# Loading the second batch's values in three pieces with tiny transfers between them

## The chip, the cores and the metric

The kernel runs on one core of a Trainium2 chip. The metric is the device time of one execution in microseconds; lower is better. Five engines work side by side: PE (TensorE, matmul), DVE (VectorE), ACT (ScalarE), POOL (GpSimd) and SP (SyncE). Sixteen DMA engines move data between HBM and the on-chip memory of 128 partitions. In this kernel POOL issues nearly all transfers, in the order of the program.

## The reference, cut to what matters

```python
# q, k, v: [8, 8, 576, 64] f32, 8 batches, 8 heads
scores = q @ k.T / 8
mask   = rel in [0, 32)                        # heads 0..3
         rel in [0, 128) and rel % 4 == 0      # heads 4..7
attn   = softmax(where(mask, scores, -1e9)) @ v
x      = attn as [4608, 512]                   # batch and position by head and dimension
logits = x @ phi                               # 32 slots: 8 experts by 4
slot_input = softmax(logits over rows).T @ x   # [32, 512]
for e in 8 experts:
    slot_out[e] = relu(slot_input[e] @ w1[e]) @ w2[e]     # 512 -> 1024 -> 512
out    = softmax(logits over slots) @ slot_out            # [4608, 512] f32
```

The values `v` of batch 1 are what the change loads in another way. `phi` is a small table of 512 by 32.

## The kernel before, in words

Everything is held in f16 on the chip; q, k, v and the weights lie in HBM as f32 and are converted on their way in, by the transfer itself. Such transfers are issued from POOL.

Attention goes batch by batch. `load_raw` (line 197) fetches Q, K or V of one batch into a tile of 128 partitions by 2304 elements: 64 rows of (head, 16 position blocks), each with two groups (the plain heads and the dilated heads), so that partition 2r + g holds row r of group g. One partition is 9216 contiguous bytes in HBM. Each of Q, K and V has two buffers. DVE transposes a raw tile in two halves (`turn`, line 223) into `qT`, `kT` or `vT`; PE makes the scores (line 273), ACT the exponentials (line 282), DVE multiplies the masks in (line 293), PE multiplies with the values (line 316), and DVE and ACT normalise (lines 328, 337, 341). A written-out list, `ORDER` (line 48), fixes the order of these steps over the batches, a few stages deep; nothing is moved by a scheduler. `logits` and the slot sums are gathered as each batch is done.

The order of the loads is fixed as well. Lines 460 to 476 issue Q and K of batch 0, V of batch 0, Q and K of batch 1, `phi_raw` and V of batch 1. From then on `loads` (line 527) issues a batch's Q, K or V two batches ahead, as soon as DVE has turned the tile whose buffer it takes; after V of batches 3 to 7 it adds one transfer of `w1` each, and after the last one all of the weights that fit: `w1` of experts 5 to 7 and `w2` of experts 0 to 2, 3 MB each as it lies on the chip. When the raw tiles are done with, `w2` of experts 3 to 5 follows (line 555), and experts 6 and 7 by halves of the columns (`load_half`, line 216).

The experts come after the last batch: PE makes the hidden layer (line 608) and `slot_out` (`emit_so`, line 635). The first halves of the columns are finished first, `so_part` is copied out of PSUM (line 652), spread and copied (line 658), and then the outputs are made: PE (line 664), ACT or DVE (lines 673, 677), and a transfer to HBM (line 686), batch by batch for the first half of the columns, then for the second, then whole rows for batches 6 and 7 and for the last 64 positions of all batches (line 713).

A transfer reports its end on one of eight completion counters, which are taken in turn. In the built program an issue on POOL waits until the transfer that used the same counter before it has landed.

Of the kernel before, what the change touches and what calls it, by code (L numbers as in the profile page):

```python
# [10 lines left out]
FP16 = mybir.dt.float16  # L11
# [16 lines left out]
N_SLOTS = 32  # L28
# [3 lines left out]
PJ = S // PB  # L32
# [12 lines left out]
    (("P", 3), ("P", 4), ("L", 0), ("L", 1), ("D", 0)),  # L45
    (("D", 1), ("D", 2), ("D", 3)),
)
ORDER = """
MD0.2 MK2.2 AP4.2 ET.3 VBc.1 S1.1 MK0.1 RP4.2 ED.3 E1.1 AD1.2 EP.3 VC.1 RD1.2 MP4.2
VCc.1 ER.3 MD1.2 AD3.2 VA.1 QT0.0 AP3.2 RD3.2 VAc.1 QT1.0 RP3.2 MD3.2 S2.1 KT1.0  # L50
# [3 lines left out]
"""  # L54
STEPS = [(w.split(".")[0], int(w.split(".")[1])) for w in ORDER.split()]
ON_ACT = ('D3', 'P0', 'P1', 'P3')
# [40 lines left out]
def kernel(  # L97
# [10 lines left out]
    nc = tc.nc  # L108
# [5 lines left out]
    consts = ctx.enter_context(tc.tile_pool(name="consts", bufs=1))  # L114
# [3 lines left out]
    ident = cst[:, o : o + 128]  # L118
    spread = cst[:, o + 128 : o + 256]
    quad = cst[:, o + 256 : o + 260]  # L120
    masks = consts.tile([128, NMASK], FP16, name="masks")
    phi_raw = consts.tile([128, 4, N_SLOTS], FP16, name="phi_raw")
    phi4 = consts.tile([128, 4, 4, N_SLOTS], FP16, name="phi4")
# [59 lines left out]
    def build_masks():  # L183
# [8 lines left out]
        for kind, i in GROUPS[1]:  # L192
            w = piece_w(kind, i)
            copies(o, lmask[i] if kind == "L" else band, w, 1)
            o += w

    def load_raw(which, b):
        t = raw_pool.tile([128, PJ * D], FP16, name=f"raw{which}_{b}", tag=f"raw{which}")
        raw[(which, b)] = t
        src = {"Q": q, "K": k, "V": v}[which][b]  # L200
        nc.gpsimd.dma_start(  # L201
            out=t, in_=src.rearrange("(g h) (p j) d -> (h p) g (j d)", g=2, j=PJ)
        )

    def load_full(t, which, e0, e1):
        if which == 1:
# [253 lines left out]
    for which in "QK":  # L460
        load_raw(which, 0)
# [3 lines left out]
    for i in range(2):  # L465
        nc.vector.memset(vX[i][:, :, :, D : D + 1], 1.0)
        for x in (xp_t[i], xd_t[i]):
            nc.vector.memset(x[:, :, 4 * D : 4 * D + 1], 1.0)
    load_raw("V", 0)
    for which in "QK":  # L470
        load_raw(which, 1)
    nc.gpsimd.dma_start(
        out=phi_raw.rearrange("p (u c) s -> p u (c s)", u=2),
        in_=moe_phi.rearrange("(u p c) s -> p u (c s)", u=2, c=2),
# [65 lines left out]
    for it in range(B + max(s for _, s in STEPS)):  # L540
        for op, stage in STEPS:
            b = it - stage
# [16 lines left out]
        if it == 0:  # L559
            nc.vector.tensor_copy(  # L560
                out=phi4, in_=phi_raw[:, :, None, :].broadcast_to([128, 4, 4, N_SLOTS])
# [55 lines left out]
    for c in range(8):  # L617
# [3 lines left out]
        out=hTm[:, 0].rearrange("p c (j s) -> p c j s", j=4)[:, :, :, 0:16], in_=hT4[:, :, :, 0:16]  # L621
    )
    nc.scalar.copy(
        out=hTm[:, 1].rearrange("p c (j s) -> p c j s", j=4)[:, :, :, 16:32], in_=hT4[:, :, :, 16:32]
# [87 lines left out]
    for e in range(2):  # L712
        nc.gpsimd.dma_start(
            out=rest[:, e, 512:576, :].rearrange("n i d -> i n d"), in_=om_l[64 * e : 64 * e + 64]
# [37 lines left out]
```

## Time and profile before

| | |
|---|---|
| runs | 178.04, 178.28, 178.61 us; median 178.28 |
| the profiled execution | 178.29 us; span 176.5 us |
| PE busy | 123.5 us (70%), 2004 matmuls |
| DVE busy | 126.0 us (71%) |
| ACT busy | 123.5 us (70%) |
| POOL busy | 38.4 us (22%) |
| DMA | 40.83 MB in 18981 packets; 62.07 MB read from HBM, 9.44 MB written |
| chain that ended last | ACT 38%, DMA 27%, DVE 14%, PE 10% |

The span is the time from the first to the last instruction in the profile; 1.8 us lie around it. The page cuts the span into 40 slices and gives, for each, the busy share of the engines in tenths and the mean busy share of the sixteen DMA engines. The chain of waits is followed back from the last instruction: at each step to what released it. The trace also keeps the times at which each transfer's sixteen shares were reported done, one by each DMA engine, and the start and length of every DMA packet, both without the engine's number. Queue q0 holds the transfers of POOL, q1 that of SP; q8 and q14 hold instructions that the engines' sequencers fetch.

### The profile page before, as it was taken

The numbers are of one execution on the slowest core, as the hardware profiler recorded it, in microseconds if no ns is written. First come the engines' busy times: TensorE is split into PE (matmuls) and PEld (weight loads), VectorE is DVE, ScalarE is ACT, GpSimd is POOL, SyncE is SP. The second block draws the span as 40 slices with busy tenths as digits, with TensorE's granted clock in tenths as the row PEclk, the third lists the DMA queues.
The fourth block names the chain that finished last, engine by engine and source line by source line (L and its number), as shares of the span: only waits on it lengthen the run. The fifth ranks groups of instructions, "written<-read, shape, count | busy, mean of one in ns | idle before, by whom it ended". The sixth has DMA issues, their size and how long they took to land.

```text
span 176.5 us, 4724 instructions
## 1 busy us (share of the span) xinstructions
PE 123.5 (70%) x2004; PEld 80.9 (46%) x2004; DVE 126.0 (71%) x275; ACT 123.5 (70%) x266; POOL 38.4 (22%) x60
## 2 busy tenths in 40 slices
PE   0026928998888888988989888978677295778300
PEld 0015616676566566656766557656332142221000
DVE  6473899999999999999999998465130104878500
ACT  6007758999999999999999999995501104888300
POOL 7321022112112112116000002710000001856600
PEclk9999999969999999999789999996858969655555
DMA  5999999999999999999999999999999999999997
GB/s 83 215 214 210 214 212 215 215 213 214 216 212 217 211 218 215 208 215 220 213 211 217 213 218 216 222 210 225 213 213 221 192 198 175 340 398 397 401 415 209
DMA packets 18981, 40.83 MB, mean 231 GB/s; under 512 B 1169, under 2 KB 11537, under 8 KB 18193
## 3 DMA queue, kind: packets, MB, share of 16 engines
q0 software_dynamic: 18816, 40.41, 113.8%
q8 instruction: 15, 0.25, 0.5%
q1 hardware_dynamic: 144, 0.14, 0.3%
q14 instruction: 6, 0.04, 0.1%
HBM read 62.07 MB, written 9.44 MB: 405 GB/s over the span
## 4 chain that ended last, share of the span: by engine, by line
ACT 38%; DMA 27%; DVE 14%; PE 10%; issue 2%; POOL 2%; POOLq 0%; ACTq 0%
DMA w<-in_moe_w_dram 19%; ACT p L282 10%; DMA phi_raw<-in_moe_phi_dram 8%; ACT vX L253 7%; ACT xp L337 7%; DVE qk L231 5%; PE f L664 5%; ACT om L673 3%; ACT xT L376 3%; ACT xT L378 3%; DVE p L293 3%; DVE vT L231 3%; ACT xd L337 2%; PE s L273 2%; PE rp L357 2%
## 5 line engine op out<-in xcount | busy, mean ns | idle before, releaser
L282 ACT ACTIVATE p<-s 128x1920 f16<-128x1920 f32 (+1 forms) x24 | 44.6, 1857 | 10.2 <-PE s L273 10.1
L273 PE MATMUL s<-qk 32*128 32x128 f16 (+2 forms) x704 | 26.7, 295 | 18.4 <-DVE qk L231 12.0
L253 ACT COPY vX<-rv 128x768 f16<-128x768 f16 (+1 forms) x32 | 27.8, 943 | 1.8 <-PE rv L247 1.8
L316 PEld LDWEIGHTS <-p 128*128 128x128 f16 (+1 forms) x480 | 22.4, 103 | 13.3 <-DVE xp L341 4.0
L337 ACT ACTIVATE xp<-o_P,rc_P 128x64 f16<-128x64 f32 x96 | 26.5, 497 | 2.2 <-DVE rc_P L328 2.2
L273 PEld LDWEIGHTS <-qk 32*128 32x128 f16 x704 | 17.3, 117 | 21.6 <-DVE qk L231 12.0
L293 DVE TENSOR_TENSOR p<-p,masks 128x1920 f16<-128x1920 f16 (+1 forms) x24 | 25.7, 1084 | 0.2
L231 DVE STREAM_TRANSPOSE qk<-rawQ 128x576 uint32<-128x576 uint32 x16 | 18.8, 1243 | 2.7 <-DMA rawQ<-in_q_dram 2.7
L316 PE MATMUL o_P<-vX,p 128*128 128x65 f16 (+1 forms) x288 | 20.0, 205 | 0.8 <-ACT xp L337 0.2
L231 DVE STREAM_TRANSPOSE qk<-rawK 128x576 uint32<-128x576 uint32 x16 | 19.5, 1231 | 0.4 <-DMA rawK<-in_k_dram 0.4
L247 PE MATMUL rv<-cst,vT 128*128 128x128 f16 x176 | 17.5, 242 | 3.2 <-DVE vT L231 1.8
L231 DVE STREAM_TRANSPOSE vT<-rawV 128x576 uint32<-128x576 uint32 x16 | 19.4, 1223 | 0.5 <-DMA rawV<-in_v_dram 0.5
L686 POOL DMA_DIRECT2D out_dram<-om x15 | 11.1, 744 | 39.2 <-DVE om L677 34.8
L247 PEld LDWEIGHTS <-vT 128*128 128x128 f16 x176 | 13.2, 124 | 7.5 <-issue 3.7
L677 DVE TENSOR_SCALAR om<-f,rrow 128x256 f16<-128x256 f32 (+1 forms) x28 | 13.5, 519 | 3.5 <-PE f L664 2.9
L664 PE MATMUL f<-so_sb,ET 32*128 32x256 f16 (+1 forms) x60 | 12.5, 392 | 3.9 <-ACT om L673 2.7
L673 ACT ACTIVATE om<-f,rrow 128x256 f16<-128x256 f32 (+1 forms) x28 | 12.8, 503 | 2.6 <-PE f L664 2.0
L376 ACT COPY xT<-rp 128x576 f16<-128x576 f16 x16 | 11.5, 909 | 1.3 <-PE rp L357 1.3
L316 PE MATMUL o_D<-vX,p 128*128 128x65 f16 x128 | 9.9, 202 | 2.5 <-DVE xp L341 2.0
L201 POOL DMA_DIRECT2D rawQ<-in_q_dram x8 | 5.1, 633 | 29.4 <-DVE rc_P L328 18.4
L378 ACT COPY xT<-rd 128x576 f16<-128x576 f16 x16 | 10.6, 795 | 0.0
L341 DVE TENSOR_TENSOR xd<-o_D,rc_D 128x256 f16<-128x256 f32 x24 | 9.9, 412 | 0.2
(81 smaller groups left out, 176.7 us busy)
## 6 DMA issues: line engine op xcount, KB each, us to landing
w<-in_moe_w_dram POOLq DMA_DIRECT2D x3, 3072.0 KB, 35.5
out_dram<-om POOLq DMA_DIRECT2D x11, 512.0 KB, 4.6
w<-in_moe_w_dram POOLq DMA_DIRECT2D x5, 1024.0 KB, 15.9
rawQ<-in_q_dram POOLq DMA_DIRECT2D x8, 576.0 KB, 12.7
rawK<-in_k_dram POOLq DMA_DIRECT2D x8, 576.0 KB, 11.4
rawV<-in_v_dram POOLq DMA_DIRECT2D x8, 576.0 KB, 11.6
out_dram<-om POOLq DMA_DIRECT2D x2, 1024.0 KB, 7.3
w<-in_moe_w_dram POOLq DMA_DIRECT2D x2, 512.0 KB, 36.7
```

The costliest lines, as they stand in the source:

```text
L231: nc.vector.transpose(out=out_, in_=in_)
L247: nc.tensor.transpose(rg[:, n_t, :, c, :], rows, ident)
L253: copy(out=vX[b % 2][:, t0 : t0 + n, :, 0:D], in_=rg.rearrange("p n h c d -> p n h (c d)"))
L273: nc.tensor.matmul(sps[:, h, c0 : c0 + w], kk, qq, start=(tt == 0), stop=(tt == 1))
L282: return nc.scalar.activation(out=pt, in_=sps[:, :, 0:n], func=AF.Exp, scale=SCALE)
L293: return nc.vector.tensor_tensor(out=pt, in0=pt, in1=m, op=ALU.mult)
L316: nc.tensor.matmul(o[rows, h, :], lhs, rhs, start=(n == 0), stop=(n == len(jobs) - 1), skip_group_check=True,)
L337: nc.scalar.activation(out=dst[:, h], in_=src[:, h], func=AF.Copy, scale=rc[:, h : h + 1])
L376: copy(out=xT_t[b][:, c, :], in_=rg[:, 0:S])
L378: copy(out=xT_t[b][:, 2 + c, :].rearrange("p (i r) -> p i r", r=DIL), in_=rg[:, :, 0:SUB].rearrange("p r i -> p i r"),)
L664: nc.tensor.matmul(fp[:, 0 : c1 - c0], ET[32 * j : 32 * j + 32, m : m + 128], so_sb[32 * j : 32 * j + 32, c0:c1], start=True, stop=True,)
L673: nc.scalar.activation(out=dst, in_=fp[:, 0 : c1 - c0], func=AF.Copy, scale=rrow[:, blk : blk + 1])
```

## The change

One load is written otherwise, that of V of batch 1. Its 128 partitions come as one transfer of 96 partitions (source rows 0 to 47 of 64, two groups each) and two transfers of 16 partitions (rows 48 to 55 and 56 to 63). After each of the three stands a tiny transfer that copies rows of `phi` into a new tile, `aside`, which nothing reads: 3, 8 and 5 rows by two pieces of 32 elements. The last count is worked out from the first, (-3 - 24) mod 16 = 5. All six are issued from POOL, where one was issued before; DVE's first transpose of this tile waits for all three pieces. What is computed stays the same.

```diff
+CURSOR = 3
...
+    aside = consts.tile([16, 3, 2, N_SLOTS + 16], FP16, name="aside")
...
+    def step_cursor(i, n):
+        nc.gpsimd.dma_start(
+            out=aside[0:n, i, :, 0:N_SLOTS],
+            in_=moe_phi[0 : 5 * n].rearrange("(p u) s -> p u s", u=5)[:, 0:4:2, :],
+        )
+
     def load_raw(which, b):
         t = raw_pool.tile([128, PJ * D], FP16, name=f"raw{which}_{b}", tag=f"raw{which}")
         raw[(which, b)] = t
         src = {"Q": q, "K": k, "V": v}[which][b]
-        nc.gpsimd.dma_start(
-            out=t, in_=src.rearrange("(g h) (p j) d -> (h p) g (j d)", g=2, j=PJ)
-        )
+        src = src.rearrange("(g h) (p j) d -> (h p) g (j d)", g=2, j=PJ)
+        if (which, b) != ("V", 1):
+            nc.gpsimd.dma_start(out=t, in_=src)
+            return
+        nc.gpsimd.dma_start(out=t[0:96], in_=src[0:48])
+        step_cursor(0, CURSOR)
+        nc.gpsimd.dma_start(out=t[96:112], in_=src[48:56])
+        step_cursor(1, 8)
+        nc.gpsimd.dma_start(out=t[112:128], in_=src[56:64])
+        step_cursor(2, (-CURSOR - 24) % 16)
```

## The prediction

> **What bounds the kernel now.** I read the page's slices first, then its queues, then the chain of waits.
>
> ```profile
> DMA  5999999999999999999999999999999999999997
> GB/s 83 215 214 210 214 212 215 215 213 214 216 212 217 211 218 215 208 215 220 213 211 217 213 218 216 222 210 225 213 213 221 192 198 175 340 398 397 401 415 209
> DMA packets 18981, 40.83 MB, mean 231 GB/s; under 512 B 1169, under 2 KB 11537, under 8 KB 18193
> ## 3 DMA queue, kind: packets, MB, share of 16 engines
> q0 software_dynamic: 18816, 40.41, 113.8%
> q8 instruction: 15, 0.25, 0.5%
> ```
>
> After its first slice the row of DMA shares is full: the sixteen DMA engines have work from 4 us to the end. 212 to 220 GB/s while f32 is read and f16 written, about 400 in the last slices, where f32 is written. Compute comes second: the chain of waits ends in one long DMA piece.
>
> ```profile
> 109.68 1.62 PE s L273 x24
> 111.30 0.28 issue
> 111.58 0.74 POOL w L220
> 112.33 34.05 DMA w<-in_moe_w_dram
> 146.41 0.32 PE so L641 x4
> 146.76 0.43 DVE so_part L652
> ```
>
> Attention's last scores are done at 111.3; then everything stands for 34 us until the second weight matrix is in. Its transfers were issued by 115 and only wait for their turn in the queue. So the time is the sum of what the **latest** DMA engine has to move, plus the tail. The tail goes with it:
>
> ```profile
> 149.40 3.03 POOL L686 DMA_DIRECT2D out_dram<-om  x4 [33.97 <-DVE om L677]
> ...
> 152.63 0.74 POOL L686 DMA_DIRECT2D out_dram<-om  x1 [0.19 <-issue]
> ```
>
> The first output is issued at 149.40, while the last weights land at 151.70 (landing times here and below are from the trace's update records). From there on half-MB outputs land every 1.31 us (153.14, 154.44, 155.79, ... 166.35), up to 175.23. The late engines go from weights to outputs without a gap, so a late engine's delay reaches the end in full.
>
> **The engines are not equally late.** For each transfer the trace records sixteen completion updates, one an engine (without the engine's number). How far the first is ahead of the last:
>
> ```
> transfer          last update   spread
> rawK, batch 1          17.89      0.41
> rawV, batch 1          20.93      0.45
> rawQ, batch 2          24.50      1.26
> rawV, batch 5          64.89      1.53
> w1 of experts 5..7    111.91      2.65
> last half of w2       151.70      2.65
> ```
>
> The first step falls on the first q8 packet, 16 KB of instructions that starts at 22.27 and takes 0.94 us: it holds up one engine. Following the packets' start times as sixteen chains, I find the first fourteen q8 packets on eight chains in a fixed turn, so six were hit twice by 129; the fifteenth (144.76) makes it seven. At 151.70 seven engines are within 0.43 us of the last (0, 0.20, 0.27, 0.28, 0.32, 0.41, 0.43), the other nine at least 1.48 before it. Those **seven late engines** set the time.
>
> **The change, part by part.** *Fewer engines for two pieces.* The 96-partition piece has 48 source rows of two groups, six partitions an engine, as before. The pieces of 16 partitions have 8 rows by 2 groups, and no transfer of before has fewer than 16 outer rows, so the trace doesn't show how such a one is spread. Bounds: over all sixteen (one partition each, nothing shifts), or over eight (two partitions each). I take eight, by the nearest rows: every transfer here with 64 or 128 outer rows gave each engine whole outer rows, and eight outer rows fill eight engines. Then, if each such transfer takes up where the one before ended, 3 + 8 + 8 + 8 + 5 = 32 brings the turn round: the first piece goes to engines 3 to 10, eight tiny rows to 11 to 15 and 0 to 2, the second piece again to 3 to 10, and the last five tiny rows to 11 to 15. Engines 3 to 10 carry two partitions more of V than before (the other eight two fewer).
> The Trainium skill ("DMA: Bandwidth & Descriptors", section on why a DMA increments its semaphore by 16) says so: the largest count up to 16 that divides the slowest dimension of both sides, and from GpSimd that many consecutive engines from a turning cursor; no row here shows it. By the same section some copies from GpSimd go to sixteen engines all the same; by that the shift would be nil, which is a rival below.
>
> *Price of the shift.* Batches 0 and 1 land at 6.84, 9.61, 12.43, 15.17, 17.89: 11.05 / 4 = 2.76 us for 8 partitions an engine, 0.345 each. Two of them: 0.69 us, plus on eight engines and minus on eight.
>
> *Price of five more transfers.* Each posts a completion on every engine: the 4-byte packets of q0 take 22 ns, so 5 x 0.022 = 0.11 us on all (from nothing, if they hide, up to 5 x 0.26 = 1.3, if each cost as much as phi_raw did from K's landing, 17.89 to 18.15; that one had 16 row pieces an engine as well, so I stay with 0.11). The tiny rows: 0.26 / 16 = 0.016 each, at most four on an engine of the second eight, 0.06.
> Sum: engines 3 to 10 get 0.69 + 0.11 = **+0.80**, the others -0.69 + 0.17 = **-0.52**.
>
> *V of batch 1 lands later.* 20.93 becomes about 21.7. It is first wanted here:
>
> ```profile
> 24.95 1.22 DVE L231 STREAM_TRANSPOSE vT<-rawV 128x576 uint32<-128x576 uint32 x1
> ```
>
> That is 3.2 us of cover left; for every later Q, K and V the cover is 6 us or more (Q of batch 2 lands at 24.50 and is turned at 31.10). With that cover gone, a late transpose would cost up to 0.8.
>
> *POOL and the eight counters.* Each transfer takes the next of eight completion counters, and in the built program an issue waits until the transfer eight before it has landed. With five more in line, Q of batch 2 no longer goes at 9.51 but waits for K of batch 1:
>
> ```profile
> 4.76 1.04 POOL L201 DMA_DIRECT2D rawV<-in_v_dram  x1
> 9.51 0.59 POOL L201 DMA_DIRECT2D rawQ<-in_q_dram  x1 [3.71 <-DVE qk L231]
> 12.27 0.59 POOL L201 DMA_DIRECT2D rawK<-in_k_dram  x1 [2.17 <-DVE qk L231]
> 15.09 0.59 POOL L201 DMA_DIRECT2D rawV<-in_v_dram  x1 [2.23 <-DVE vT L231]
> 22.08 0.59 POOL L201 DMA_DIRECT2D rawQ<-in_q_dram  x1 [6.40 <-DVE qk L231]
> ```
>
> So Q goes at 17.9, K behind it at 18.5, V at 20.3, when the 96-partition piece has landed; Q of batch 3 keeps its 22.1. The first transfer had packets moving at 2.68 after its issue at 1.28, 1.4 us. Q's rows are thus ready at 19.3. The relieved engines run out of V at 20.48 - 0.52, about 19.9, the others at 21.2. Margin 0.6 us: cost nothing, with up to 0.6 or so on the relieved engines if it fails.
>
> **Which engines are the late ones?** This decides the sign. If the latest engine is among 3 to 10, the end moves by +0.80. If it is not but one of the other six is, by 0.80 less 0.20 to 0.43, so +0.37 to +0.60. Only if all seven are among the relieved eight, it moves by -0.52 (the next group, 1.48 earlier, then stands at -0.68, behind). The trace gives no numbers. The eight chains are hit in an order that fits eight engines in a row; of sixteen places where such a row could start, one puts all seven into the relieved eight. Weak evidence besides: packets of equal start stand in the record in an order that never contradicts itself between two chains, and in it three chains that are never hit stand ahead of most of the eight. If that order is the engines' numbers, the row starts at 3 or above and does not wrap, and overlaps 3 to 10.
>
> **Rivals.**
> Forecast: at least one late engine is loaded, +0.37 to +0.80. I take +0.66: 178.29 + 0.66 = **178.95**. Chance 0.58.
> Other side, *the relieved eight are the late ones*: 178.29 - 0.52 = 177.77. For it: eight are hit and eight are relieved, so an exact match is possible; against it: one place in sixteen and the record's order. It decides as soon as all seven are outside 3 to 10. Chance 0.22, more than a sixteenth, since the numbering is unknown to me.
> *The change doesn't do what it says*: pieces go over sixteen engines, only five completions and the tiny rows are added, +0.11 to +0.17: 178.43. Chance 0.15.
> *The queue runs dry at Q of batch 2*, because the counters hold it to 17.9 and packets need longer than 2 us from there: all engines lose 0.5 to 1.0 at about 20 us, 179.0 to 179.3, whatever the sets. Against it: 1.4 us at the start. Chance 0.05.
>
> **Numbers.** The sum is made against the profiled execution, 178.29 (span 176.5 and 1.8 around it), next to the median of 178.28. A measurement of this kernel tells about 0.3% (0.53 us) from no change. Of the forecast's 0.58, about 0.10 lies below 178.82 and counts as same, 0.48 is slower; of the 0.22, 0.14 is counted faster and 0.08 same; the third is same; the fourth mostly slower. Faster 0.14, same 0.33, slower 0.53. The range must reach to the gain, as without it 0.22 is left out: 177.7 to 179.2. The forecast's own: 178.6 to 179.1.
>
> **What would show it.** Landing of V of batch 1: spread of about 1.8 (0.45 + 2 x 0.69) instead of 0.45 if eight engines are used; 0.45 if sixteen. POOL's issue of Q of batch 2 at 17.9 with a wait on DMA. No gap in the DMA row near 20 us. The last w2 half: first and last update; at 152.2 to 152.5 in the forecast, 151.2 in the gain. The chain's w piece longer or shorter by the same, the tail unchanged. I am wrong if these landings move and the end doesn't, or if compute waits on V of batch 1.

## The result, and the profile after

The changed kernel takes 178.97 us (median of 13 runs, 178.71 to 179.85) against 178.26 (13 runs, 177.95 to 178.71): ratio 1.0042, 95% interval 1.0026 to 1.0058. It is slower by about 0.7 us, as forecast (178.95). Its profiled execution took 179.09 us (span 177.3), the one before 178.29 (span 176.5). Six of its thirteen runs lie at 178.71 to 178.80, so what is read below from one execution at 179.09 need not hold in full for all of them. In twice_same, a run below, two of six executions were slow, near 182.5 us, and its ratio is made of the other four.

The page of the changed kernel, the rows that answer to those of before:

```profile
DMA  5999999999999999999999999999999999999997
GB/s 89 211 214 209 193 214 212 214 213 216 216 212 217 212 214 215 214 214 213 215 211 219 212 218 216 225 213 213 224 213 211 199 198 171 318 399 395 402 412 218
DMA packets 19188, 40.84 MB, mean 230 GB/s; under 512 B 1376, under 2 KB 11744, under 8 KB 18400
## 3 DMA queue, kind: packets, MB, share of 16 engines
q0 software_dynamic: 19024, 40.41, 113.5%
q8 instruction: 15, 0.25, 0.5%
```

Between its first and last slice the row of DMA shares still shows nothing but nines, but the row below it shows a change: the fifth slice (17.7 to 22.2 us) moved 193 GB/s, 214 before. The bytes are the same to 0.01 MB; 207 small packets have come in.

The end of the chain of waits of the changed kernel (start, us, what):

```profile
138.87 2.68 issue
141.55 6.13 PE so L656 x60
147.70 0.43 DVE so_part L667
148.18 0.28 PE rep L672
148.48 0.38 ACT so_sb L673
```

`so_part` is copied at 147.70, 146.76 before. In this execution PE is itself busy up to there: it ran the stretch 141 to 147 us at half the clock (granted 0.50, 0.73 before). Is PE then the cause? A run below, with the same landings, has PE free for 0.97 us ahead of them and gains nothing by it.

Landings are from the trace's update records, last update and spread of the sixteen, in us:

```
transfer                              before          after
V of batch 1, 96 partitions                           20.21  0.50
  rows 48 to 55                                       20.74  0.66
  rows 56 to 63 (before: the whole)   20.93  0.45     21.80  1.36
Q of batch 2                          24.50  1.26     25.17  1.79
w2, last of the first halves          146.37 2.66     147.29 3.25
w2, last of the second halves         151.70 2.65     152.11 2.73
last output                           175.23          176.01
```

The last output is 0.78 later, the last weights only 0.41. The first halves of the columns, for which `so_part` waits, are 0.92 later: so the loss has two parts, and the second (some 0.37 us) goes back to a landing just before 147.3. POOL's first issues of outputs in the changed kernel:

```profile
150.35 2.19 POOL L701 DMA_DIRECT2D out_dram<-om  x3 [34.00 <-DVE om L692]
152.74 0.75 POOL L701 DMA_DIRECT2D out_dram<-om  x1 [0.20 <-ACT om L688]
```

They begin 0.95 later than before (149.40). The first output packets start at 151.63, 0.48 us before the last weights are in; before it was 150.68, 1.02 ahead. Around 153.1 the DMA engines then run dry for a moment: from 152.5 to 153.5 their packets leave 0.12 us an engine unused (before 0.00), and the third output lands 1.44 us after the second (1.30 before). So a part of the second loss is seen in the packets; the rest builds up over the later outputs.

POOL's issues at the start of the changed kernel, from its timeline (in brackets the idle time ahead and what ended it):

```profile
4.80 0.96 POOL L213 DMA_DIRECT2D rawV<-in_v_dram  x1
5.33 1.01 POOL L200 DMA_DIRECT2D aside<-in_moe_phi_dram  x1
7.15 0.57 POOL L215 DMA_DIRECT2D rawV<-in_v_dram  x1 [0.81 <-DMA rawQ<-in_q_dram]
9.91 0.56 POOL L200 DMA_DIRECT2D aside<-in_moe_phi_dram  x1 [2.19 <-DMA rawK<-in_k_dram]
12.73 0.55 POOL L217 DMA_DIRECT2D rawV<-in_v_dram  x1 [2.26 <-DMA rawV<-in_v_dram]
15.48 0.58 POOL L200 DMA_DIRECT2D aside<-in_moe_phi_dram  x1 [2.21 <-DMA rawQ<-in_q_dram]
18.46 0.59 POOL L211 DMA_DIRECT2D rawQ<-in_q_dram  x1 [2.40 <-DMA phi_raw<-in_moe_phi_dram]
19.02 0.66 POOL L211 DMA_DIRECT2D rawK<-in_k_dram  x1
20.74 0.58 POOL L211 DMA_DIRECT2D rawV<-in_v_dram  x1 [1.06 <-DMA aside<-in_moe_phi_dram]
22.09 0.58 POOL L211 DMA_DIRECT2D rawQ<-in_q_dram  x1 [0.77 <-DVE qk L246]
```

By the eight counters, Q of batch 2 waits for K of batch 1 (landed at 17.90), and goes at 18.46 (9.51 before), 0.56 us later. The bracket names `phi_raw` (18.15), the landing that came last, but in no_middle, a run below, the same issue waits for Q of batch 1 (15.00) and goes at 15.55, with no other landing near. The pieces and tiny transfers follow their landings by 0.28 us (6.87 and 7.15, 15.20 and 15.48). From 22.09 on the times are those of before. The packet records show what this did: per 0.342 us, 16 rows of 9 KB should start, one an engine. From 19.37 on it is 9, 14, 10, 13, 12, 14, 15 and then 16 again (before: 16 with single 15s). 25 rows are missing, 25 x 0.345 / 16 = 0.54 us an engine on average, less what the tiny rows and the added completions took. The relieved engines' last rows of V start by 19.26 and take 0.36 us; the first rows of Q, from 19.80, take up to 1.1 us. The engines that still had pieces of V did not stop.

DVE's first transpose of this tile did not move; from its timeline:

```profile
24.96 1.22 DVE L246 STREAM_TRANSPOSE vT<-rawV 128x576 uint32<-128x576 uint32 x1
```

### The profile page after: what moved, and what is told of

Read it like the earlier page. It is cut to its first block, busy times and chain, and to the rows that moved or that the text cites. A ratio compares the mean times of both kernels' runs of the same rounds, so it can differ in the third digit from the quotient of the medians.

```text
span 177.3 us, 4730 instructions
## 1 busy us (share of the span) xinstructions
PE 124.3 (70%) x2004; PEld 80.8 (46%) x2004; DVE 125.9 (71%) x275; ACT 123.6 (70%) x266; POOL 41.3 (23%) x65
## 4 chain that ended last, share of the span: by engine, by line
ACT 43%; PE 21%; DVE 16%; DMA 8%; issue 4%; POOL 2%; POOLq 0%; ACTq 0%; DVEq 0%
ACT p L297 10%; ACT xp L352 9%; DMA phi_raw<-in_moe_phi_dram 8%; ACT vX L268 8%; DVE qk L246 5%; ACT xT L391 5%; PE f L679 5%; ACT xT L393 4%; PE so L656 4%; ACT om L688 3%; PE hps L623 3%; ACT xd L352 3%; DVE vT L246 3%; PE rv L262 2%; DVE p L308 2%
## 5 line engine op out<-in xcount | busy, mean ns | idle before, releaser
L262 PE MATMUL rv<-cst,vT 128*128 128x128 f16 x176 | 18.2, 250 | 3.1 <-DVE vT L246 1.8
L246 DVE STREAM_TRANSPOSE qk<-rawK 128x576 uint32<-128x576 uint32 x16 | 19.6, 1235 | 0.4 <-DMA rawK<-in_k_dram 0.4
L262 PEld LDWEIGHTS <-vT 128*128 128x128 f16 x176 | 13.8, 126 | 7.2 <-issue 3.8
L352 ACT ACTIVATE xd<-o_D,rc_D 128x64 f16<-128x64 f32 x32 | 9.2, 536 | 1.3 <-DVE rc_D L343 1.3
```

What stands on the lines that cost most here:

```text
L246: nc.vector.transpose(out=out_, in_=in_)
L262: nc.tensor.transpose(rg[:, n_t, :, c, :], rows, ident)
L352: nc.scalar.activation(out=dst[:, h], in_=src[:, h], func=AF.Copy, scale=rc[:, h : h + 1])
```

## The experiments

The theory behind the forecast: the latest DMA engines set the end, and some of them are among engines 3 to 10, which carry two partitions more. Its rivals: the transfers themselves cost the time, or the hold-up of Q of batch 2. Ratios are against the kernel before on the same chip, with the 95% interval.

### Without the shift: the middle tiny transfer left out, and pieces over sixteen engines

Run no_middle: the second piece begins where the first one ended.

```diff
-        step_cursor(1, 8)
...
-        step_cursor(2, (-CURSOR - 24) % 16)
+        step_cursor(2, (-CURSOR - 16) % 16)
```

> The three pieces of V and two of the three tiny transfers stay; the middle one is gone and the last has 13 rows, so the two pieces of 16 partitions go to engines 3 to 10 and then 11 to 2, two partitions to every engine. Theory (the loss is the uneven load): four more transfers than before, 4 x 0.022 = 0.09 us on every engine, so about +0.1 us against the kernel before, V of batch 1 lands with a spread near 0.5 us. Rival (the loss is the price of many transfers and of the held-up issue of Q of batch 2): +0.5 to +0.7 us, like the changed kernel.

Measured: 178.47 against 178.29, ratio 1.0016 (1.0007 to 1.0025). The second piece lands with a spread of 0.25 us, the first one in two groups of eight with 0.47: the two pieces fill up all sixteen engines. The last weights land at 151.68. Four more transfers, without the shift, leave the late landings where they were; the medians are 0.18 apart.

Run sixteen: three pieces and three tiny transfers, all of 16 or more rows.

```diff
+        nc.gpsimd.dma_start(out=t[0:64], in_=src[0:32])
+        step_cursor(0, 16)
+        nc.gpsimd.dma_start(out=t[64:96], in_=src[32:48])
+        step_cursor(1, 16)
+        nc.gpsimd.dma_start(out=t[96:128], in_=src[48:64])
+        step_cursor(2, 16)
```

> Six transfers as in the change, but each has 16, 32 or more outer rows: V as 64, 32 and 32 partitions, the tiny ones with 16 rows. Theory (uneven load): every engine keeps its 8 partitions, five more completions cost 0.11 us, so +0.1 to +0.2 us. Rival (the number of transfers and the eight counters, which hold Q of batch 2 back to 18 us, cost the time): +0.5 to +0.8 us, and the DMA engines stand idle near 20 us.

Measured: median 178.55, ratio 1.0029 (1.0009 to 1.0049; two of twelve runs lie above 179.7). Q of batch 2 is issued at 18.25 here as well, but no engine had run out of V; last weights 151.68. The hold-up by itself, with all engines equally loaded, moves no landing of the last weights (the median is 0.26 over that of before). The first halves, though, land 0.39 late (146.76); more of that below.

### Other engines loaded: counts 11 and 15

```diff
-CURSOR = 3
+CURSOR = 11
```

> The mirror image: engines 11 to 15 and 0 to 2 carry two partitions more, 3 to 10 two fewer. In the changed kernel's landings the first, sixth, seventh and eighth of the eight engines hit by code fetches were loaded and the second to fifth relieved. Theory (four of the late engines stand on either side): the latest engine is now among the loaded, +0.8 us at the last weights, and the time 0.6 to 0.9 us over the kernel before. Rival (the change only picked the wrong side): -0.5 us.

> Engines 15 and 0 to 6 carry two partitions more, 7 to 14 two fewer. Theory A (the engines hit by code fetches are a row of eight, and 3 to 10 overlapped its first four, so it is 7 to 14): all late engines are relieved, the last weights land 0.5 us earlier than before and the time is 0.3 to 0.5 us under the kernel before, less what the relieved engines lose standing idle near 20 us. Theory B (they are every second engine): four of them are loaded again, +0.5 us. Theory C (the row is 15 to 6): all are loaded, +0.8 us.

Measured: 11 gives 179.21, ratio 1.0066 (1.0040 to 1.0092), last weights 152.38 (+0.68, for 0.8 expected). 15 gives 178.73, ratio 1.0030 (1.0018 to 1.0042), last weights 152.22. So loading the other eight engines is slower too, and so is a set between them: the theory that the eight chains with the instruction fetches are eight engines in a row, which count 15 would relieve, falls. The last landings fit every second engine instead, visited in a turn: any eight in a row then hold four of them. In before the late engines end about 0.43, 0.28, 0, 0.29, 0.27 and 0.39 us ahead of the last, in the order of their first fetch (the seventh 0.4 after its second, the eighth 1.53). With 3 the groups of landings put the first, sixth, seventh and eighth among the loaded: -0.39 + 0.80 = +0.41. With 11 it is the second to fifth: 0 + 0.80; with 15 the fourth to seventh: -0.27 + 0.80 = +0.53. Measured: +0.41, +0.68, +0.52. The spread bears this out for two of the counts: with 3, three engines end within 0.01 us of each other and the next 0.50 ahead; with 11, four end within 0.13 and the next 0.77 ahead. With 15 there are no such groups (six engines within 0.18), so there the fit rests on the last update alone. The engines' numbers themselves are not in the trace.

### The dose: the shift twice, and opposed

V of batch 4 is loaded in the same way, with the count c = 3 (twice_same) or c = 11 (twice_opposed).

```diff
-        if (which, b) != ("V", 1):
+        if (which, b) not in (("V", 1), ("V", 4)):
...
+        c, i = (3, 0) if b == 1 else (11, 3)
```

> The change made twice, in V of batch 1 and in V of batch 4, with the same counts 3, 8, 5: engines 3 to 10 carry four partitions more. Theory (late engines that carry more set the end, and half of those that fetch are among them): two shares of 0.80 on a late engine that was 0.39 ahead of the last: last weights at 151.70 - 0.39 + 1.60 = 152.9, with a spread of over 4 us, and the time 179.5 to 180.0 (178.3 + 1.2, and up to 0.5 more by the fetch). Rival (what costs is the hold-up of Q of batch 2 by the completion counters at 18 to 21 us, which batch 4 does not have): the second time adds no more than its five transfers, 179.0 to 179.2.

> The same ten transfers more as in the run with the change made twice, but with the counts 11, 8, 13 in V of batch 4, so that engines 11 to 2 carry the two partitions more there: over both, every engine carries what it carried before. Theory of the late engines: only the transfers remain, 2 x 0.11 to 2 x 0.17 us: 178.5 to 178.65 (up to 178.9 if the fetch comes in between), the spread of the last weights back to 2.6. Rival (the hold-up at 18 to 21 us costs): 179.0 to 179.3, since V of batch 1 is as in the changed kernel.

Measured: twice_same has ratio 1.0073 (1.0057 to 1.0089), 179.60 in the profiled execution, last weights at 152.94 (152.9 expected) with a spread of 3.98. The dose is as the theory has it, and the rival (only transfers added) falls. Its chain shows the weights longer by that much:

```profile
112.29 30.00 DMA w<-in_moe_w_dram
142.31 5.69 PE so L657 x59
```

The piece of DMA ends at 142.29, when w2 of experts 3 to 5 is in; 141.10 before.

twice_opposed missed the theory's figure: ratio 1.0054 (1.0039 to 1.0069), median 179.28, last weights 152.88. The opposed shift did not cancel. Either the second set was not the complement of the first, or the relief of the first had been lost. The landings speak for the second. At Q of batch 2 the engines of after without a fetch stand in two groups: seven around 24.12 and eight around 23.5, where before all stood around 23.45. The loaded ones are thus +0.67, in place of +0.80, and the relieved ones +0.05, in place of -0.52.

### The same away from the hold-up

late_opposed makes the two opposed shifts in V of batches 4 and 5, batch4_only the single shift in batch 4.

```diff
-        if (which, b) != ("V", 1):
+        if (which, b) not in (("V", 4), ("V", 5)):
```

> The pieces and tiny transfers in V of batches 4 and 5 in place of batch 1, counts 3, 8, 5 and then 11, 8, 13: engines 3 to 10 carry two partitions more by the one and two fewer by the other. Theory H: in the run with batches 1 and 4 the opposed shift did not cancel, because in batch 1 the eight relieved engines stood idle from 19.5 to 21.5 us until Q of batch 2 was issued, so that their relief was lost (+0.07 in place of -0.52 at 25 us) and only the load of the others remained. Here the queue is full, so the two shifts cancel and only ten transfers remain, 2 x 0.11 to 2 x 0.17 us: last weights at 151.9 to 152.05 with a spread of 2.5 to 2.8, 178.5 to 178.65 us (up to 0.3 more if the 15th fetch falls into the first half's last weights). Rival G (the second set of engines is not the complement of the first: the turn does not stand at 0 at batch 4): last weights over 152.4 and 179.1 to 179.5, as in that run.

> The change's six transfers with 3, 8, 5 in V of batch 4 in place of batch 1, so no queue runs dry. Theory (late engines 0.39 behind the last are loaded): last weights at 151.70 - 0.39 + 0.80 = 152.1, 178.7 to 179.0, and the late engines among the relieved keep their relief: they end 0.9 to 1.2 ahead of the last (0.6 in the changed kernel). Rival (the hold-up of Q of batch 2 is what costs): 178.35 to 178.45, only the transfers being left.

Measured: late_opposed has its last weights at 151.92 with a spread of 2.61, as theory H said; the rival G needed over 152.4. So the sets are complements, and ten transfers cost 0.22, 0.022 each. The profiled execution took 178.58, as expected, but the median is 178.76, above it: the eight runs lie in two groups, 178.50 to 178.58 and 178.94 to 179.08, ratio 1.0028 (1.0016 to 1.0040).

batch4_only: 178.80, ratio 1.0035 (1.0023 to 1.0047), last weights 152.22 (+0.52; 0.41 was expected). Without any hold-up the shift costs the same, so the rival (178.35 to 178.45) falls. Behind three engines within 0.24 of the last, the next end 0.85 ahead of it (0.9 to 1.2 expected for the relieved ones, 0.50 in the changed kernel), which fits engines that kept their relief. The medians say less than the landings: ten balanced transfers (178.76) cost about as much as five with the shift (178.80). That the shift is what costs rests on the traced executions. Its chain of waits:

```profile
113.02 33.91 DMA w<-in_moe_w_dram
146.93 0.04 issue
146.97 0.32 PE so L656 x4
```

The first halves land at 146.93, 0.56 later than before, and the last output at 175.74, 0.51 later: here all three move by one amount, as the forecast had it. In the changed kernel they do not.

### The second part: PE's 15th instruction fetch

In the changed kernel this fetch (145.19) comes while its engine still has rows of the last of the first halves to move; the engine's share lands 1.5 us later than by its place among the others, 0.49 us after all of them. One transfer later it is delayed by 1.0 only. To shift the fetch, 32 PE instructions were added (after_code, before_code) or left out (after_less, before_less, whose hidden layer lacks a quarter of its rows) in a stretch where PE waits for weights anyway.

```diff
-    for c in range(8):
+    for c in 3 * list(range(8)):
         nc.tensor.transpose(hT[:, c, :], h_sb.rearrange("p (q l) -> p l q", l=8)[:, c, :], ident)
```

> The changed kernel, with the eight PE transposes of the hidden layer (hT, at about 138 us) done three times over: 32 PE instructions more, in a stretch in which PE waits for weights, so that PE's 15th instruction fetch (16 KB on q8, at 145.19 us) is asked for one to two microseconds earlier in the weights. Theory T: of the +0.92 us by which the last weights of the first half of the columns are later (147.29 for 146.37), 0.49 are not the shift of partitions but that fetch, which reaches its DMA engine while the engine still has a piece of this transfer to do; the end follows this landing. Then without the coincidence it lands at 146.8 to 146.9, the last weights stay at 152.1, and the time is 0.3 to 0.5 below the changed kernel's: 178.5 to 178.7, against 178.3 before. Rival R: the place of the fetch is of no account and the tail follows the last weights (152.11) or the compute: 178.9 to 179.0.

> The kernel before with the same 32 PE instructions more. In it the 15th fetch reaches its engine when that engine is through with the first half's last weights (it is 1.5 us ahead), so both theories expect no change: 178.2 to 178.4, the last weights of the first half at 146.4 and the last of all at 151.7. It tells what the added instructions cost by themselves.

Measured: before_code 179.19, ratio 1.0048 (1.0034 to 1.0062); after_code 180.19, ratio 1.0126 (1.0087 to 1.0165). Both expectations missed, for a reason that I had not thought of. The page of before_code:

```profile
GB/s 89 208 216 209 215 216 212 215 215 212 214 215 217 211 213 218 214 212 216 215 213 214 216 214 226 217 211 218 222 209 216 194 197 167 386 398 392 405 414 139
...
q8 instruction: 16, 0.26, 0.5%
```

There are 16 fetches, and the last one comes at 161.25, among the outputs. The last weights are not late (151.46), fifteen engines report the last output from 174.48 to 174.97 (before: from 174.64 on), and the sixteenth 0.97 us after them, at 175.94: a spread of 1.46 in place of 0.59. The kernel is slower by that. It is the plainest proof in this study that the latest engine sets the end: 1.07 us of one engine, where none has slack, cost 0.8. For the question asked the pair is of no use: in after_code the 15th fetch came at 145.04, hardly earlier, and the first halves at 147.10.

```diff
-            for dc in range(4):
+            for dc in range(3):
```

> The changed kernel with 32 PE instructions fewer: the hidden layer is summed over three quarters of its 512 rows (the last quarter's 16 matmuls and 16 weight loads are left out), at about 131 to 136 us, where PE is ahead of the weights. PE's 15th instruction fetch then comes later in the weights than at 145.19 us, and no 16th comes (the run with 32 more got one at 162 us, on an engine without slack, and lost 0.8 us by it). Theory T: the fetch reaches its engine when that is through with the last weights of the first half; these land at 146.8 (147.29 with the fetch in between, 146.37 before), and the time is 178.5 to 178.75. Rival R (the place of the fetch is of no account): 178.9 to 179.0.

> The kernel before with the same 32 PE instructions left out (hidden layer over three quarters of its rows). Both theories: 178.2 to 178.4, first half at 146.4, last weights at 151.7; it tells what leaving them out does by itself.

Measured: before_less 178.21, ratio 0.9998 (0.9989 to 1.0007). after_less 178.81, ratio 1.0035 (1.0023 to 1.0047); the fetch came at 145.18, not later, and the first halves at 147.28. So neither pair moved the fetch in the changed kernel by more than 0.15 us, and theory T was not put to the test that I meant. after_less does settle PE's share; from its timeline:

```profile
141.55 4.80 PE L656 MATMUL so<-w,hTm 128*32 128x512 f16 x57 [2.69 <-issue]
147.32 0.29 PE L656 MATMUL so<-w,hTm 128*32 128x256 f16 x4 [0.97 <-DMA w<-in_moe_w_dram]
```

PE stood idle for 0.97 us and then waited for the landing all the same, at a ratio within the interval of the changed kernel's (1.0042). The landing is the bound there, not PE.

What remains is a comparison over the profiled executions, without the two that had a sixteenth fetch. The fetch shows as a spread that is larger in the last of the first halves than in the transfer ahead of it:

```
                spread ahead, of it   last weights   last output   difference
after           2.72  3.25            152.11         176.01        23.90
sixteen         2.49  2.92            151.68         175.45        23.77
cursor11        3.07  3.64            152.38         176.30        23.92
after_less      2.54  3.07            152.08         175.93        23.85
before          2.65  2.66            151.70         175.23        23.53
no_middle       2.59  2.56            151.68         175.15        23.47
cursor15        2.56  2.62            152.22         175.71        23.49
twice_same      3.98  4.01            152.94         176.47        23.53
twice_opposed   3.52  3.56            152.88         176.43        23.55
late_opposed    2.61  2.64            151.92         175.46        23.54
batch4_only     3.14  3.18            152.22         175.74        23.52
before_less     2.47  2.49            151.52         175.10        23.58
```

In the four with the larger spread the end comes 23.77 to 23.92 after the last weights, in the eight others 23.47 to 23.58, whatever else was changed. So some 0.3 to 0.4 us of the loss go with that coincidence. That it is the cause is shown by no run that makes or takes it away alone; that stays open. The two groups of late_opposed, 0.5 us apart, would fit it, but only one execution was traced.

## Why the prediction was right, point by point

**The latest DMA engine sets the end.** Held: a double dose gave +1.24 on the last weights (+1.21 by the sum), and one fetch among the outputs 0.8 us at the end.

**Eight engines for a piece of 8 rows by 2.** Held. The pieces land in two groups of eight (0.66, then 1.36 of spread; 1.8 was forecast), and without the middle transfer they balance to 0.25. The Trainium skill ("DMA: Bandwidth & Descriptors", "Why a DMA increments its semaphore by 16 and not by 1") states both the eight engines and the turning start, and these landings agree with it. Its exception, sixteen engines for some copies, did not come up.

**Two partitions, 0.69 us, and five transfers, 0.11.** Held in the main: together +0.67 on the loaded engines at Q of batch 2, for 0.80. The price of a transfer is not settled: 0.022 for each of ten in late_opposed, but nothing on the last weights for four in no_middle and five in sixteen (both 151.68).

**The margin of 0.6 us at Q of batch 2.** Failed. The landing that the issue waits for was the one forecast, K of batch 1 at 17.90, but the issue came 0.56 us after it, at 18.46, where the text put nothing in between. The 1.4 us to the first packets held (19.80), but the relieved engines were through with V at about 19.6, not 19.9. They ran dry and lost their relief (+0.05 in place of -0.52). The rival of the dry queue (chance 0.05) thus came true on half of the engines. The text had this case, "with up to 0.6 or so on the relieved engines if it fails", and it cost nothing, because the loaded engines set the end; sixteen and batch4_only bear that out. Had the relieved eight been the late ones, the forecast gain of 0.52 would have been gone by this alone.

**V of batch 1.** Held: 21.80 (21.7 forecast), transposed at 24.96 as before.

**Which engines are late.** The sign held, "if it is not but one of the other six is, by 0.80 less 0.20 to 0.43": the latest loaded engine had been 0.39 ahead of the last, and +0.41 was measured. I chose +0.66, between the two cases, which was 0.25 too much. The weak evidence from the order of the records pointed the right way, but the eight are not a row: the one row that 15 would have relieved is ruled out by that run. If they are every second engine, as the three counts fit, any eight in a row load four of them, and the rival with the gain (chance 0.22) could not come true for any count.

**The tail.** Failed as it stood: "a late engine's delay reaches the end in full", over the last weights. The end follows the first halves of the columns, which `so_part` waits for; mostly they move with the last weights, but here they were 0.92 late against 0.41. This added some 0.37 in the traced execution. So the sum of 178.95 came out because one term was 0.25 too large and another, of about 0.37, was missing: the mechanism was right, the agreement to 0.02 us was luck.

## What to carry to other kernels

When the DMA engines are the bound, look at the sixteen landing times of a transfer and not at its last: a row full of nines hides engines 2.6 us apart, and moving load between engines gained nothing in any run here, as each run that moved it loaded some of the late ones. Count completions as well as bytes: a few tiny transfers issued from the same queue can hold the next large one until its engines are empty. And when a sum fits, check its terms one by one: here two errors of about 0.3 us cancelled.

## What the runs showed of the hardware

Instruction fetches take DMA time from data: a 16 KB packet on q8 took 0.88 to 1.09 us of one engine, with fifteen of them the spread of the landings grew from 0.45 to 2.65 us, and 32 PE instructions more brought a sixteenth and 0.8 us. The Trainium skill ("Runtime: NRT & Kernel Launch", "Instruction fetch mechanics") says that instructions come in blocks of 16 KiB over the sequencer's own DMA queue and that the cost is mostly hidden. The packets agree with the first. Whether PE ever waited for a block was not examined; for the DMA engine that carries it, the time is not hidden here.

Adding or leaving out 32 PE instructions ahead of it moved the 15th fetch by only 0.15 and 0.01 us in the changed kernel (in the one before by 0.69 and 0.18); why it stayed was not found.
